# The last product of a gated block, formed by one level of Strassen on pairs of token tiles

## The chip, the cores and the metric

The kernel runs on one core of a Trainium2 chip. The metric is the time of one execution on the device in microseconds (us); less is better. A core has TensorE (PE: matmuls, with their weight loads shown apart as PEld), VectorE (DVE), ScalarE (ACT), GpSimd (POOL) and SyncE (SP), which issues the DMA transfers here. Each engine takes its instructions in the order in which they stand in its queue and waits on semaphores.

## What is computed

Two branches work on the same normalised input, and their product is added to it (S = 2048 tokens, D = 576, Fh = 2304):

```python
xn = _layernorm(x, axis=-1)
s = _A_ref(xn, A_wqkv, A_wo)          # 32 heads, sliding window of 256, then @ wo
# _B_ref:
z = _gelu(xn @ w_in)                  # [S, 2 * Fh]
z1 = z[..., :Fh]
z2 = _layernorm(z[..., Fh:], axis=-1)
g = jnp.einsum("ts,bsf->btf", w_sp, z2) + b_sp[None, :, None]
b = jnp.einsum("bsf,fd->bsd", z1 * g, w_out)     # the last product
return x + s * _silu(b)
```

All inputs are float32. The kernel splits every float32 operand into a high part h (rounded to the matmul format by ACT) and a low part l (the rest, by a subtraction), and forms a product of two operands as three matmuls: h h, h l, l h. This is what `split` does.

## The kernel before

The kernel goes through its stages one after the other; TensorE has work in all of them.

- First come the projections and attention (the first half of the span), the product with `wo`, and at the side the first product of the gate branch. Its results lie in DRAM: `z1_d`, `z2_d`, and the attention branch's result in `s_d`.
- **The spatial stage** (L1205 to L1430) multiplies `w_sp` with z2. It already uses one level of Strassen: `PRODUCTS` names seven products of 1024 x 1024 blocks. The features go in three groups g of 384; per group there are 7 products n, each in 8 steps s of 128 rows, so `order_sp` holds 168 steps m. A step is 18 matmuls of 128x512 into six PSUM banks `acc`. `load_w` fetches the `w_sp` operand four steps ahead, `split_step` splits it two steps ahead. `evict` adds a product's banks to the running sums when its last step (s = 7) is done, and queues the gate's remaining work in `lazy`: loads of z1, Gelu, the multiplication with z1, and the stores of the result y = z1 * g into `y_d` (features on rows, tokens on columns). `run_lazy(4)` takes four of these in each step.
- In the last group w_out is made ready at the side: `wout_unit` loads one of its 18 row blocks (128 x 576) and splits it. The places are buffers that the spatial stage no longer needs (`w_place`, `last_weights`). `y_ahead` and `y_second` do the same with the first two token tiles of y.
- **The out stage** (L1432 to L1494) takes the 16 token tiles in eight chunks of two. `load_y` loads a chunk of y (256 tokens, 1 KB pieces) and splits it. For each token tile there are 18 feature blocks x 3 matmuls of the split x 2 halves of 288 output columns, all 128x288, accumulated in two PSUM banks (`po`). Four such pairs of banks are in rotation, so a tile's banks are read while the next tile's are filled. `finish_half` then applies Silu, multiplies with a row block of `s_d`, adds x, and the result is stored.

The spatial stage's order on all engines is the order of the program (`manual_schedule`); in the out stage a planner had set it. SP's queue, too, is one queue: a transfer that waits for its buffer holds back all later ones.

The lines of the profile that the text uses: L1396 the spatial matmuls (`acc`), L1489 the out-stage matmuls (`po`), L114 and L115 the two halves of `split` (ACT, DVE), L1345 and L1326 sums and multiplication of the gate, L1332 the stores to `y_d`, L1445 the loads of y, L1476 to L1478 the three steps of `finish_half`. L684, L270 and L836 to L840 are GpSimd's additions in earlier stages.

Of the kernel before, what the change touches and what calls it, by code (L numbers as in the profile page):

```python
# [9 lines left out]
F32 = mybir.dt.float32  # L10
# [6 lines left out]
P = 128  # L17
# [47 lines left out]
def kernel(  # L65
# [30 lines left out]
    s_d = dram.tile([S, D], F32, name="s_d")  # L96

# [115 lines left out]
    raws, halves, wpools = {}, {}, []  # L213

# [19 lines left out]
    with ExitStack() as early:  # L234
# [889 lines left out]
        wpools.append(open_pool(ctx, "w0p", side="right"))  # L1124
        with ExitStack() as ph:
# [39 lines left out]
            for n in range(NS):  # L1165
# [26 lines left out]
                if n == 13:  # L1192
                    thirds.close()
                    wpools.append(open_pool(ctx, "sprp", bufs=2, side="right"))
# [9 lines left out]
    zq = open_pool(ctx, "zq")  # L1204
    with ExitStack() as ph:  # L1205
        wpools.append(open_pool(ph, "wsp", bufs=2, side="right"))
        wk = open_pool(ph, "wk", bufs=2)
        accp = open_pool(ph, "accp", space=PSUM)
# [9 lines left out]
        wos = {}  # L1218
        wbufs = []
        y_first, y_raw = {}, []  # L1220

        def y_ahead():

            raws = []

            def load(j):
                raw = wk.tile([P, 512], F32, name=f"u2{j}", bufs=1).rearrange("p (f t) -> p f t", t=P)
                n = min(4, FH // P - 4 * j)
                sp.dma_start(raw[:, :n], y_d[4 * j * P:(4 * j + n) * P, 0:P].rearrange("(f p) t -> p f t", p=P))
                raws.append((raw, n))  # L1230

            def form(j):
                raw, n = raws[j]
                for i in range(n):
                    f = 4 * j + i
                    c0 = 4 * D + f % 3 * 2 * P
                    h, l = (wbufs[f // 3][:, c0 + a * P:c0 + a * P + P] for a in range(2))
                    split(h, l, raw[:, i])
                    y_first[f] = (h, l)

            return [partial(load, j) for j in range(5)], [partial(form, j) for j in range(5)]

        def wout_unit(f, place):

            def load():
                raw = wk.tile([P, D], F32, name="wr")
                sp.dma_start(raw, w_out[f * P:(f + 1) * P, :])
                return raw

            def form(raw):  # L1250
                hl = place()
                for h in hl[0]:
                    w = h.shape[-1]
                    c0 = 0 if h is hl[0][0] else 288
                    act.activation(h, raw[:, c0:c0 + w], AF.Copy)
                whole = [tuple(h[:, a * 288:a * 288 + 288] for a in range(2)) if len(hs) == 1 else hs
                         for hs in map(tuple, hl) for h in hs[:1]]
                for l in hl[1]:
                    w = l.shape[-1]
                    c0 = 0 if l is hl[1][0] else 288  # L1260
                    if w == D and len(hl[0]) == 1:
                        dve.tensor_tensor(l, raw, f32(hl[0][0]), ALU.subtract)
                    else:
                        for a in range(c0 // 288, (c0 + w) // 288):
                            b = a * 288
                            dve.tensor_tensor(l[:, b - c0:b - c0 + 288], raw[:, b:b + 288], f32(whole[0][a]),
                                              ALU.subtract)
                wos[f] = whole

            return load, form  # L1270

        def w_place(n, k, i):

            if i == 0:
                wbufs.append((xp if k < 5 else zc).tile([P, 8 * ZW], F32R, name=f"b{k}"))
            return [[wbufs[n][:, (2 * i + a) * D:(2 * i + a + 1) * D]] for a in range(2)]

        places = []

        def last_place(i):  # L1280
            if not places:
                places.extend(last_weights())
            return places[i]

        def last_weights():

            r = [w_tile(len(order_sp) + n, [P, 1024], F32R, "spr") for n in range(3)]
            h, l = (w_tile(len(order_sp), [P, 1024], F32R, t) for t in ("sph", "spl"))
            z = w_tile(len(order_sp), [P, ZW], F32R, "zh")
            lead, rest = slice(0, D), slice(D, D + 288)  # L1290
            return [([r[0][:, lead]], [r[1][:, lead]]), ([r[2][:, lead]], [h[:, lead]]),
                    ([l[:, lead]], [r[0][:, rest], r[1][:, rest]]),
                    ([r[2][:, rest], h[:, rest]], [l[:, rest], z[:, :288]])]

        def y_second():

            for j in range(6):
                raw = zq.tile([P, ZW], F32, name="zr", bufs=ZRB).rearrange("p (f t) -> p f t", t=P)
                sp.dma_start(raw, y_d[3 * j * P:3 * (j + 1) * P, P:2 * P].rearrange("(f p) t -> p f t", p=P))
                y_raw.append(raw)  # L1300

        def tiles(name):
            return [wk.tile([P, 512], F32, name=f"{name}{j}", bufs=1) for j in range(6)]
# [262 lines left out]
```

## Time and profile before

| | |
|---|---|
| median of 3 runs | 1881.53 us (1880.1 to 1881.65) |
| the profiled execution | 1876.21 us, span 1874.5 us |
| mean granted TensorE clock | 0.997 |
| busy: PE, PEld, DVE, ACT, POOL | 98%, 86%, 56%, 49%, 21% |
| spatial stage | about 953 to 1640 us |
| out stage | 1640 to 1870 us, 1728 matmuls |

The busy share of PE says little by itself: matmuls are pipelined, so that one of 295 ns starts every 133 ns, and their durations overlap. What counts is the distance between starts and whether TensorE waits. The share on the chain of waits is a better guide. POOL has no work after the first half of the span.

### The profile page before, as it was taken

Reading aid. Unit: us, or ns where it says so; the run is one execution under the profiler, and the core shown is the slowest. Engines: PE = TensorE matmul, PEld = TensorE weight load, DVE = VectorE, ACT = ScalarE, POOL = GpSimd, SP = SyncE. Lnnn points to the kernel's source line nnn. Section 1 sums busy time; section 2 is a strip of 40 time slices with the busy share of each in tenths; the row PEclk is TensorE's granted clock in tenths of the full one; section 3 lists DMA queues with packets and bytes.
Section 4 is the critical chain, followed back from the end, with each engine's and each line's share of the span. In section 5 each row is a group of like instructions: output and inputs, shape, how many; then the busy total and the mean of one; then the engine's idle time right before and its main releaser. Section 6 shows DMA issues by size and latency. Waiting matters only on the chain.

```text
span 1874.5 us, 38529 instructions
## 1 busy us (share of the span) xinstructions
PE 1845.2 (98%) x14552; PEld 1613.9 (86%) x14552; DVE 1040.6 (56%) x2273; ACT 914.3 (49%) x1760; POOL 399.8 (21%) x487
## 2 busy tenths in 40 slices
PE   8999999999999999999999999999999999999999
PEld 8999999997777777776988888888888888899998
DVE  6311333457766776751257686667857666653322
ACT  5523222315666676666467655565465434532221
POOL 3332333434465455554000000000000000000000
PEclk8999999999999999999999999999999999999999
DMA  7895688886566676655867668566586547765441
GB/s 250 205 231 164 229 288 280 287 273 192 161 193 168 174 200 181 181 144 171 259 226 255 237 218 291 210 230 203 197 285 204 192 144 230 252 215 168 135 134 60
DMA packets 234314, 389.85 MB, mean 208 GB/s; under 512 B 51984, under 2 KB 145680, under 8 KB 234000
## 3 DMA queue, kind: packets, MB, share of 16 engines
q1 hardware_dynamic: 234128, 387.39, 65.8%
q8 instruction: 114, 1.87, 0.4%
q14 instruction: 72, 0.59, 0.1%
HBM read 274.74 MB, written 111.78 MB: 206 GB/s over the span
## 4 chain that ended last, share of the span: by engine, by line
PE 87%; DVE 4%; DMA 3%; SPq 2%; ACT 2%; issue 1%; POOL 0%; POOLq 0%; DVEq 0%; ACTq 0%
PE acc L1396 34%; PE po L1489 12%; PE mb L205 11%; PE ma L669 6%; PE mb L669 5%; PE ma L205 5%; PE ops L750 4%; PE tps L722 3%; PE sp L598 3%; PE wops L1155 2%; SPq L361 1%; DMA st_d<-qkhl 1%; DMA att<-st_d 1%; PE ma L378 1%; DVE junk L602 1%
## 5 line engine op out<-in xcount | busy, mean ns | idle before, releaser
L1396 PE MATMUL acc<-spl,zh 128*128 128x512 f32 x1008 | 392.6, 389 | 0.8 <-DVE spl L115 0.6
L1396 PE MATMUL acc<-sph,zh 128*128 128x512 f32 x1008 | 392.2, 389 | 0.0
L1396 PE MATMUL acc<-sph,zl 128*128 128x512 f32 x1008 | 392.2, 389 | 0.0
L602 DVE CUSTOM_DVE_ANT_0 junk<-sp,band 128x384 bf16<-128x384 f32 (+1 forms) x512 | 276.2, 540 | 111.6 <-PE sp L598 32.9
L726 ACT ACTIVATE pt<-tps 128x384 f32<-128x384 f32 (+2 forms) x576 | 231.3, 441 | 120.4 <-PE tps L722 76.5
L669 PE MATMUL mb<-b,z1wh 64*128 64x512 f32 x648 | 224.7, 399 | 1.0 <-ACT z1o L674 0.6
L1396 PEld LDWEIGHTS acc<-spl,zh 128*128 128x128 f32 x1008 | 189.2, 188 | 41.7 <-DVE spl L115 2.4
L669 PE MATMUL ma<-b,z1wh 64*128 64x512 f32 x648 | 223.8, 397 | 0.6 <-ACT zt L946 0.4
L1396 PEld LDWEIGHTS acc<-sph,zl 128*128 128x128 f32 x1008 | 189.2, 188 | 39.2
L1396 PEld LDWEIGHTS acc<-sph,zh 128*128 128x128 f32 x1008 | 189.2, 188 | 39.1
L115 DVE TENSOR_TENSOR spl<-spr,sph 128x1024 fp32r<-128x1024 f32 x168 | 205.4, 1223 | 30.0 <-ACT sph L114 29.0
L114 ACT ACTIVATE zh<-b 128x384 fp32r<-128x384 f32 x168 | 87.4, 520 | 228.8 <-PE acc L1396 228.6
L722 PE MATMUL tps<-att 56*128 56x384 f32 (+1 forms) x576 | 176.6, 344 | 2.8 <-DMA att<-mhl 1.3
L115 DVE TENSOR_TENSOR zl<-b,zh 128x384 fp32r<-128x384 f32 x168 | 93.1, 554 | 152.0 <-ACT zh L114 152.0
L114 ACT ACTIVATE sph<-spr 128x1024 fp32r<-128x1024 f32 x168 | 175.8, 1047 | 0.6 <-DMA spr<-in_w_sp_dram 0.5
L598 PE MATMUL sp<-att 54*128 54x384 f32 (+1 forms) x512 | 160.8, 348 | 2.1 <-DVE mx L602 2.1
L1489 PE MATMUL po<-b,yh 128*128 128x288 f32 x840 | 147.2, 295 | 0.5 <-ACT gs L1476 0.5
L669 PE MATMUL ma<-b,z1wl 64*128 64x512 f32 x324 | 128.0, 395 | 0.0
L669 PE MATMUL mb<-b,z1wl 64*128 64x512 f32 x324 | 127.4, 393 | 0.0
L722 PEld LDWEIGHTS tps<-att 56*128 56x128 f32 x576 | 99.4, 184 | 30.9 <-issue 9.0
L1489 PEld LDWEIGHTS po<-b,yh 128*128 128x128 f32 x840 | 124.1, 188 | 0.7 <-ACT gs L1476 0.7
L669 PEld LDWEIGHTS ma<-b,z1wh 64*128 64x128 f32 x648 | 117.2, 186 | 6.9 <-ACT z1o L674 1.8
(229 smaller groups left out, 4163.3 us busy)
## 6 DMA issues: line engine op xcount, KB each, us to landing
spr<-sc_d SPq DMA_DIRECT2D x96, 512.0 KB
spr<-in_w_sp_dram SPq DMA_DIRECT2D x72, 512.0 KB
zr<-z_d SPq DMA_DIRECT2D x144, 192.0 KB
z_d<-zt SPq DMA_DIRECT2D x48, 384.0 KB
z_d<-z1o SPq DMA_DIRECT2D x72, 256.0 KB
z1t<-z_d SPq DMA_DIRECT2D x72, 256.0 KB
y_d<-z1t SPq DMA_DIRECT2D x72, 256.0 KB
a<-in_w_sp_dram SPq DMA_DIRECT2D x64, 256.0 KB
```

Source lines behind the costliest of these rows:

```text
L114: act.activation(hi, src, AF.Copy)
L115: dve.tensor_tensor(lo, src, f32(hi), ALU.subtract)
L205: pe.matmul(banks[h][:, :n], *both[h][i], start=i == 0, stop=i == STEPS - 1)
L598: pe.matmul(ps[:, :w], q_of(u, j)[0:54, i * P:(i + 1) * P], k_of(u, j)[0:54, k0:k0 + w], start=True, stop=True)
L602: dve.tensor_tensor_reduce(out=junk[:, :w], in0=ps[:, :w], in1=band[:, m0:m0 + w], scale=1.0, scalar=-3.0e38, op0=ALU.add, op1=ALU.max, ac ...
L669: pe.matmul(ps, w, x_, start=n == 0, stop=n == STEPS - 1)
L722: pe.matmul(ps[:, :m * P], k_of(u, j)[:, (kb - base) * P:(kb - base + 1) * P], q_of(u, j)[:, (a - lo) * P:(a - lo + m) * P], start=True, s ...
L726: act.activation(pt[:, j, d0:d0 + n * P], ps[:, (qa - a) * P:(qa - a + n) * P], AF.Exp, scale=scale)
L750: pe.matmul(o_ps[c][32 * j:32 * j + 32, (qa - 4 * c) * P:(hi - 4 * c + 1) * P], vgs[u][:, kb - k0, j * VW:j * VW + 32], pt[:, j, (qa - kb) ...
L1155: pe.matmul(po[:, i, :288], lt[:, cs], r[:, i * 288:(i + 1) * 288], start=n == 0, stop=n == len(pl) - 1)
L1396: pe.matmul(acc[j], z[:, ps], w[:, cs], start=s == i == 0 and n in OPENS, stop=s == 7 and i == 2, skip_group_check=True)
L1489: pe.matmul(po[i][:, a, :288], y if ahead else y[:, i * P:(i + 1) * P], w[a], start=f == 0 and m == 0, stop=f == NF - 1 and m == 2)
```

## The change

The last product is formed by one level of Strassen (in Winograd's form). A pair p is made of two token tiles t and t + 4; y is cut into quarters a11, a12 (tile t, first and second half of the features) and a21, a22 (tile t + 4), w_out into four quarters of 1152 x 288. Instead of eight products of quarters there are seven, in the order `W_ORDER` = P4, P1, P2, P6, P7, P5, P3, each 9 feature blocks x 3 matmuls of 128x288.

- The four sums of weight quarters are formed by GpSimd in group 1 of the spatial stage (`t_load`, `t_form`, `t_store`) and stored to DRAM as `t_d`.
- The seven weight operands are 63 blocks of 128 x 288. `w_fetch` loads five at a time (tiles 0 to 12), `w_halve` splits them: ACT forms the high part, DVE or, where `pool` is given, GpSimd the low part. Tiles 0 to 6 are halved in group 2 of the spatial stage, tile 7 in its last step, tiles 8 to 12 during the first two products of the out stage.
- `y_load` loads a quarter of a pair in three transfers (128 tokens, 512-byte pieces); `y_form` splits a product's operand (three pieces of 384 columns) and has GpSimd form the sums of quarters in place: six additions after P4's split, three after P1's, three after P2's.
- In PSUM, P2 is added onto P1's bank, P7 onto P6's and P3 onto P5's. `total` reads a bank after its product: ACT copies P4 and P1 to SBUF (`t4`, `t1`), DVE adds the others to running sums. `end` applies Silu and the rest to a quarter of the output; `load_end` loads the rows for it two quarters ahead.
- After each product i, the order on every engine's queue is: `total(i)`, `formed(i + 3)` (the split for the product three further, and the load of the next pair's quarter that takes its buffer), at i = 0 and 1 the weights, then `end`.
- The whole out stage is now in program order as well.

In the diff below the removed functions (`y_ahead`, `wout_unit`, `w_place`, `last_place`, `last_weights`, `y_second`, and the old out stage) are cut.

```diff
...
+        def t_form(t, n):
+            b11, b12, b21, b22 = (t[:, m, :n] for m in range(4))
+            pool.tensor_tensor(b11, b12, b11, ALU.subtract)
+            pool.tensor_tensor(b12, b22, b12, ALU.subtract)
+            pool.tensor_tensor(b22, b22, b11, ALU.subtract)
+            pool.tensor_tensor(b21, b21, b22, ALU.subtract)
...
+        W_ORDER = ("P4", "P1", "P2", "P6", "P7", "P5", "P3")
+        W_SUMS = {"P5": 0, "P6": 1, "P7": 2, "P4": 3}
+        W_PARTS = {"P1": (0, 0), "P2": (1, 0), "P3": (1, 1)}
...
+        def w_fetch(i, home):
+            n = 3 if i == 12 else 5
+            raw = (home.tile([P, 2304], F32, name=f"o{i % 2}") if home is yw else
+                   home.tile([P, 1440], F32, name="wr", bufs=2))
...
+        def w_halve(i, home, name, low=dve):
+            raw = w_raws.pop(i)
+            n = raw.shape[1]
+            t = home.tile([P, 8 * ZW if home in (xp, zc) else n * D], F32R, name=name)[:, :n * D]
+            t = t.rearrange("p (a k c) -> p a k c", a=2, c=288)
+            act.activation(t[:, 0], raw, AF.Copy)
+            low.tensor_tensor(t[:, 1], raw, f32(t[:, 0]), ALU.subtract)
+            w_tiles.append(t)
...
+        QUADS = ("a11", "a21", "a22", "a12")
+        OF = {"P4": "a22", "P1": "a11", "P2": "a12", "P6": "a11", "P7": "a21", "P5": "a22", "P3": "a12"}
...
+        def y_form(i, p, prod):
+            home = yw if i % 3 < 2 else homes["o2"]
+            o = home.tile([P, 2304], F32R, name=f"o{i % 3}", bufs=1).rearrange("p (a f t) -> p a f t", a=2, t=P)
+            src = quads[p, OF[prod]]
+            for n in range(3):
+                split(o[:, 0, 3 * n:3 * n + 3], o[:, 1, 3 * n:3 * n + 3], src[n])
+            operands[p, prod] = o
+            q = {name: quads.get((p, name)) for name in QUADS}
+            if prod == "P4":
+                for n in range(3):
+                    pool.tensor_tensor(q["a22"][n], q["a21"][n], q["a22"][n], ALU.add)
+                    pool.tensor_tensor(q["a21"][n], q["a11"][n], q["a21"][n], ALU.subtract)
...
             if s == 7:
-                evict(g, n)
+                evict(g, n, acc)
             load_w(m + 4)
             split_step(m + 2)
...
+            if g == 1 and n < 5:
+                k0, w = 2 * n, 1 if n == 4 else 2
+                if s == 1:
+                    t_now = t_load(k0, w)
+                if s == 3:
+                    t_form(t_now, w)
+                if s == 6:
+                    t_store(t_now, k0, w)
...
+                if n == 6:
+                    if s == 2:
+                        y_load(0, "a11")
+                        y_load(0, "a21")
+                    if s == 3:
+                        y_load(0, "a22")
+                        y_load(0, "a12")
+                    if s in (5, 6):
+                        y_form(s - 5, *SEQ[s - 5])
...
+        OPEN_OF = {"P4": "P4", "P1": "P1", "P2": "P1", "P6": "P6", "P7": "P6", "P5": "P5", "P3": "P5"}
...
+        def product(i):
+            p, prod = SEQ[i]
+            key = p, OPEN_OF[prod]
+            begin = key not in banks
+            if begin:
+                banks[key] = outp.tile([P, 512], F32, name=f"c{len(opened) % 8}", bufs=1)
+                opened.append(key)
+            o = operands.pop((p, prod))
+            for k in range(9):
+                wh, wl = w_block(prod, k)
+                for n, (y, w) in enumerate(((o[:, 0, k], wh), (o[:, 0, k], wl), (o[:, 1, k], wh))):
+                    pe.matmul(banks[key][:, :288], y, w, start=begin and k == n == 0, stop=k == 8 and n == 2,
+                              skip_group_check=True)
+            return banks[key][:, :288]
...
+        for i in range(len(SEQ)):
+            c = product(i)
+            done = total(i, c)
+            formed(i + 3)
+            if i == 0:
+                w_halve(8, right, "w0", pool)
+                w_fetch(9, right)
+                w_fetch(10, right)
+                run_lazy(len(lazy))
+                gates.close()
+                yp = open_pool(ph, "yp")
+                for _ in range(2):
+                    load_end()
+                w_halve(9, right, "w1", pool)
+                w_fetch(11, right)
+            if done is not None:
+                end(i, done)
+                load_end()
+            if i == 1:
+                w_halve(10, yp, "w2")
+                w_fetch(12, right)
+                w_halve(11, yp, "w3", pool)
+                w_halve(12, yp, "w4", pool)
```

306 lines of the change are left out of this document (144 added, 162 removed).

## The prediction

> **What bounds the kernel now.** I read the page first, then the chain of waits, then the last 250 us as a timeline and in windows. The page:
>
> ```profile
> span 1874.5 us, 38529 instructions
> ```
> ```profile
> PE 87%; DVE 4%; DMA 3%; SPq 2%; ACT 2%; issue 1%; POOL 0%; POOLq 0%; DVEq 0%; ACTq 0%
> ```
> ```profile
> L115 DVE TENSOR_TENSOR spl<-spr,sph 128x1024 fp32r<-128x1024 f32 x168 | 205.4, 1223 | 30.0 <-ACT sph L114 29.0
> L114 ACT ACTIVATE zh<-b 128x384 fp32r<-128x384 f32 x168 | 87.4, 520 | 228.8 <-PE acc L1396 228.6
> ```
> ```profile
> L115 DVE TENSOR_TENSOR zl<-b,zh 128x384 fp32r<-128x384 f32 x168 | 93.1, 554 | 152.0 <-ACT zh L114 152.0
> L114 ACT ACTIVATE sph<-spr 128x1024 fp32r<-128x1024 f32 x168 | 175.8, 1047 | 0.6 <-DMA spr<-in_w_sp_dram 0.5
> ```
>
> TensorE carries 87% of the chain. The end of that chain is the stage that is rewritten, and one window inside that stage:
>
> ```profile
> 1640.20 222.22 PE po L1489 x1674
> ```
> ```profile
> 1862.91 7.47 PE po L1489 x54
> ```
> ```profile
> 1740.00:1760.00 20.00, 20.00 (x153) 20.00 (x152) 8.79 (x14) 6.39 (x10) 0.00 (x0) 1.00 0.55 178
> ```
>
> The output product is 1728 matmuls back to back: 222.22/1674 = 0.1327 us from start to start, with DVE 44% busy, ACT 32%, POOL idle and the clock at 1.00. Nothing else is late there, so the stage (229.7 us) is worth exactly its matmul count. The profiled execution took 1876.2 us, 1.7 more than its span; the median of the runs shown is 1881.5, 5.3 above it. I make the sum against the profiled time and add the change to the median.
>
> **What is removed.** 16 token tiles x 18 x 3 x 2 = 1728 matmuls become 8 pairs x 7 products x 27 = 1512 of the same 128x288 shape, each with its own weight load as before. 216 x 0.1327 = 28.7 us less. One product is 27 x 0.1327 = 3.58 us.
>
> **What is added inside each pair.** Before, a product had its own two banks and nobody had to empty them in time. Now P2 adds onto P1's bank, P7 onto P6's and P3 onto P5's, and each must wait until ACT (t1) or DVE has read the bank, straight after its last matmul. The end of the kernel shows such a reading, and step 167 of the spatial stage shows TensorE released by DVE:
>
> ```profile
> 1870.08 0.29 PE L1489 MATMUL po<-sph,yl 128*128 128x288 f32 x1
> 1870.40 0.41 ACT L1476 ACTIVATE gs<-po 128x288 f32<-128x288 f32 x1 [7.55 <-PE po L1489]
> 1870.85 0.46 DVE L1477 TENSOR_TENSOR fs<-fs,gs 128x288 f32<-128x288 f32 x1 [7.01 <-ACT gs L1476]
> ```
> ```profile
> 1634.75 1.22 DVE L115 TENSOR_TENSOR spl<-spr,sph 128x1024 fp32r<-128x1024 f32 x1 [0.39 <-ACT sph L114]
> ```
> ```profile
> 1636.03 0.19 PEld L1396 LDWEIGHTS acc<-spl,zh 128*128 128x128 f32 x1 [0.32 <-DVE spl L115]
> ```
>
> The next matmul would have started at 1870.21; ACT reads 1870.40 to 1870.81, TensorE resumes 0.06 later: 0.65 us lost. With DVE's 0.46 it is 0.70. Before P3 DVE has also to finish P7's two sums, P4's three subtracts and P7's multiply and add; that is 2 x 0.46 + 3 x 0.48 (next rows) + 2 x 0.46 = 3.3, with the waits for ACT's copies and Silu between them about 4, against the 3.58 of P5: I take 0.5 more. 0.65 + 0.70 + 1.20 = 2.55 us a pair, 20.4 us in all. Bounds: 2.05 a pair (16.4) if DVE is always free; above, the port rival below.
>
> Each pair also has 21 splits of 384 columns, 12 POOL adds, 12 loads of y, 8 row loads, 4 stores:
>
> ```profile
> 1652.10 2.60 ACT L114 ACTIVATE yh<-zr 128x384 fp32r<-128x384 f32 x6 [1.36 <-DVE z1t L1326]
> 1652.91 2.90 DVE L115 TENSOR_TENSOR yl<-zr,yh 128x384 fp32r<-128x384 f32 x6
> ```
> ```profile
> L684 POOL TENSOR_TENSOR z1wl<-z1raw,z1wh 128x384 fp32r<-128x384 f32 x51 | 51.1, 1025 | 6.7 <-ACT z1wh L684 6.7
> ```
> ```profile
> L270 POOL TENSOR_TENSOR wql<-wraw,wqh 128x1152 fp32r<-128x1152 f32 x13 | 34.7, 2677 | 60.4 <-ACT wqh L267 49.1 <-DVE xpair L318 9.9 <-ACT qkhl L114 1.4
> ```
>
> ACT: 21 x 0.43 + 6 readings of 0.41 = 11.5 us. DVE: 21 x 0.48 + 13 x 0.46 = 16.1. POOL: 12 x 1.02 = 12.3. A pair lasts 7 x 3.58 + 2.55 = 27.6 us, so on totals these lie beside TensorE and cost nothing more.
>
> **The start of the stage.** This is the dear place. Weights 7 to 12 are no longer formed under the spatial stage: their fetch and halving stand in the queues of SP, ACT, DVE and POOL during the first pair, in program order, and ahead of the bank readings. The rows for the walk:
>
> ```profile
> 1642.97 3.67 DVE L1345 TENSOR_TENSOR cb<-acc,t 128x512 f32<-128x512 f32 x6
> ```
> ```profile
> 1647.97 2.49 DVE L1326 TENSOR_TENSOR z1t<-z1t,cb 128x512 f32<-128x512 f32 x4
> 1648.68 4.49 SPq L1332 DMA_DIRECT2D y_d<-z1t  x6
> ```
> ```profile
> 1656.19 1.45 SPq L1445 DMA_DIRECT2D yr<-y_d  x3
> ```
> ```profile
> 1659.46 0.85 ACT L114 ACTIVATE yh<-yr 128x768 fp32r<-128x768 f32 x1 [4.76 <-DMA yr<-y_d]
> ```
> ```profile
> 1662.01 1.28 ACT L1476 ACT_TABLE_LOAD   x1
> ```
> ```profile
> 1632.00:1634.00 2.00, 2.00 (x11) 1.65 (x10) 0.20 (x1) 1.91 (x4) 0.00 (x0) 1.00 1.11 346
> ```
>
> Prices: an issue on SP 0.48; transfer at 0.35 MB/us; landing 1.7 after transfer (3.27 from issue to use, less 0.48 and 393 KB/0.35 = 1.1). Halving 1440 columns: by the 384 and 1024 rows ACT 1.39, DVE 1.66; by the 384 and 1152 rows POOL 3.30.
>
> Time 0 is the end of the spatial stage (1640.0). DVE came free of the last split at -4.0. It then does nine operand subtracts (4.3, and about 2 for POOL's adds beside them), weight 7 (1.7), the six sums of the last gate (3.7), four multiplies (2.5) and P6's three subtracts (1.5): 11.7. Only these free the buffers of a11, so SP issues the next pair's a11 until 13.1 and weight 9's fetch until 13.6. 0.59 + 0.74 MB from 12.2 on take 3.8 us; it lands at 17.7. ACT halves it (19.1), and only behind that reads P1's bank (19.5). P2 was due at 2 x 3.58 + 0.65 = 7.8: **11.7 us late**. P2 and P6 end at 26.7. Meanwhile SP issues weight 10, six stores (4.5) and four row loads until 21; weight 11 waits for POOL's low half of weight 9 (19.1 + 3.3 = 22.4) and goes out by 22.9, three loads of a21 by 24.3, weight 12 by 24.8. These 1.77 MB, from 22.9 on, have landed at 29.7. ACT halves weight 12 (0.9), copies P5's operand (1.3), loads its table (1.3), does Silu (0.4); DVE multiplies and adds (0.9) and only then reads P6's bank (0.5): P7 starts at 35.0, due at 27.4: **7.6 late**. Together 19.3 us. Before, sums, multiplies and stores of the last gate ran on until 1653 as well (rows above), under matmuls that waited for none of it; that cover is gone, because P2 and P7 wait for engines which have this work ahead. Bounds: 2 if the weights land before ACT reaches them, 32 if every landing takes half as long again and POOL slows DVE throughout.
>
> TensorE's own clock follows such pauses:
>
> ```profile
> 10.00:15.00 5.00, 2.98 (x38) 2.62 (x40) 2.86 (x8) 2.57 (x5) 2.62 (x2) 0.65 0.66 261
> 15.00:20.00 5.00, 5.00 (x62) 5.00 (x64) 3.55 (x11) 3.26 (x7) 2.72 (x3) 0.67 0.58 203
> ```
>
> After 2 us of idleness the granted clock is 0.65 and 0.67. In five us at 0.67 a third is lost, 1.7 us. The first pause pays nothing, since P7 waits for the weights anyhow; the second pays 1.7. The Trainium skill, "TensorE: Matmul & The Clock Gate", Part 1, says that an idle window of about 3.4 us puts the clock to half until a busy window has passed. By that rule the estimate is the same 1.7 for each pause.
>
> **Smaller edits.** The sums of w_out on GpSimd lie in group 1 of the spatial stage, five times four adds of up to 576 columns and 40 transfers; DVE there is
>
> ```profile
> 1301.00:1376.00 75.00, 75.00 (x333) 62.12 (x332) 54.57 (x80) 39.79 (x60) 0.00 (x0) 1.00 0.61 207
> ```
>
> 73% busy and the DMA engines 61%, which hides them; the seven weights halved in group 2 take places that w_out's rows had. But the last split already came 0.32 us late (row above) and now has six y loads more ahead on SP: +1, between 0 and 5. The last product has one DVE sum more: +0.5.
>
> **Sum.** -28.7 + 20.4 + 19.3 + 1.7 + 1 + 0.5 = +14.2 us: 1890.4 for the profiled execution, 1895.7 for the median.
>
> **Rivals.** *The start is covered* (the other side). If weights 9 to 12 land before ACT's queue reaches them, the start costs 2, and with the lower bound for the banks -28.7 + 16.4 + 2 + 0.5 = -9.8: 1871.7 for the median. It decides once the start costs under 8. For it: DMA rows of 0.35 MB/us and buffers that may come free sooner than I walk; against it: the order on SP, which has a11's loads ahead of weight 9.
>
> *DVE and POOL hold each other up.* Around 228 us, where both work, the trace shows it:
>
> ```profile
> 223.58 1.47 DVE L115 TENSOR_TENSOR z2w<-z1wl,z2w 128x384 fp32r<-128x384 f32 x3
> ```
> ```profile
> 227.53 3.78 DVE L115 TENSOR_TENSOR z2w<-z1wh,z2w 128x384 fp32r<-128x384 f32 x3
> ```
> ```profile
> 227.84 1.49 POOL L837 TENSOR_TENSOR a<-a,a 128x512 f32<-128x512 f32 x1
> ```
> ```profile
> 244.82 1.29 POOL L836 TENSOR_TENSOR a<-a,a 128x512 f32<-128x512 f32 x1 [12.36 <-DMA a<-in_w_sp_dram]
> ```
>
> Beside POOL's adds three subtracts take 3.78 instead of 1.47. If that meets P4's subtracts and P7's multiply and add in every pair, the reading of P5's bank comes 2.3 us later, 8 x 2.3 = 18 more than the forecast: 1914. Against it: POOL's six adds start only behind those subtracts. The Trainium skill, "SBUF — State Buffer", section Who interferes with whom, says that a VectorE instruction with two SBUF inputs and a GpSimd one that reads SBUF exclude each other for a whole instruction. The trace agrees in part: DVE slows to 39%, POOL only to 87%.
>
> **How the numbers follow.** A measurement of this kernel tells about 0.2%, 3.8 us, from no change. The forecast (start 12 to 28 us late) has 0.58, the port rival 0.14, a start that costs 4 to 8 and ends near zero 0.08, the covered start 0.20. So faster 0.20, same 0.08, slower 0.72. The forecast alone reaches from 1886 to 1905. The range goes down to the covered start at 1873 and up to 1911, leaving out its lower half and most of the port rival.
>
> **What would show it.** Right: about 1512 matmuls at 0.133; in the first pair, pauses of near 12 us before P2 and 8 before P7; then pairs of 27 to 28 us with three pauses of 0.6 to 1.3 each, released by ACT and DVE. Wrong: a first pair under 35 us, pauses in the spatial stage over 5 us, or later pairs over 29 us.

## The result, and the profile after

| | before | after |
|---|---|---|
| median of 4 runs beside each other | 1880.82 us (1879.06 to 1881.65) | 1926.01 us (1920.23 to 1929.66) |
| ratio | | 1.0239, interval 1.0212 to 1.0266 |
| the profiled execution | 1876.21 us, span 1874.5 | 1929.66 us, span 1928.0 |

The changed kernel is 2.4% slower, 45 us; forecast were 14 us slower. 1926.0 lies above the range (1873 to 1911). The sign was right, the size was not.

The page of the changed kernel, its span, busy times, granted clock by slices and chain:

```profile
span 1928.0 us, 38834 instructions
...
PE 1840.4 (95%) x14336; PEld 1601.7 (83%) x14336; DVE 1184.4 (61%) x2404; ACT 960.1 (50%) x1872; POOL 561.0 (29%) x607
...
PEclk9999999999999999999999999999999999789999
...
PE 83%; DVE 7%; DMA 4%; issue 3%; ACT 2%; SPq 1%; POOL 0%; DVEq 0%; ACTq 0%; POOLq 0%
```

PE is on 83% of the chain instead of 87%, DVE on 7% instead of 4%. The out stage (L1503 here, operation `c`) begins at 1647.4 and lasts 280.6 us to the end of the span; before, it began at 1640.0 and lasted 234.5: 46.1 more. The spatial stage lasts 688.5 us instead of 687.4; the rest of the 53.5 us between the two spans is a spatial stage that begins 6.3 us later (958.9 instead of 952.6). The edit leaves the work up to there as it was, and the other kernels of this study began it at 952.4 to 957.8: that part is put down to the spread between executions.

The out stage on TensorE, as a timeline: start, time, engine, line, operation, count, and in brackets the wait ahead of the group and what ended it. The first pair and the two after it:

```profile
1647.37 7.29 PE L1503 MATMUL c<-b,o 128*128 128x288 f32 x54
1674.21 9.22 PE L1503 MATMUL c<-b,o 128*128 128x288 f32 x54 [19.55 <-ACT t L1511]
1693.15 3.22 PE L1503 MATMUL c<-b,o 128*128 128x288 f32 x12 [9.71 <-DVE u2s L1516]
...
1705.55 5.38 PE L1503 MATMUL c<-w,o 128*128 128x288 f32 x27 [2.50 <-DVE u3s L1525]
...
1718.58 7.40 PE L1503 MATMUL c<-b,o 128*128 128x288 f32 x54 [0.50 <-ACT t L1511]
1726.62 1.83 PE L1503 MATMUL c<-b,o 128*128 128x288 f32 x12 [0.64 <-ACT o L115]
...
1736.51 5.26 PE L1503 MATMUL c<-w,o 128*128 128x288 f32 x27 [2.51 <-DVE u3s L1525]
...
```

The pauses stand where the forecast had put them: before P2 (ACT's copy of P1's bank), before P7 (DVE's u2s; for 1726.62 the profile names the last semaphore, an operand of ACT, but DVE read the bank just then) and before P3 (u3s). The first pair is far too long, and the later ones take 30.7 to 31.0 us from P3 to P3 (1736.51 - 1705.55 = 31.0), not 27.6. The wait of 2.51 was put at 1.20, and behind it the 27 matmuls of P3 are shown with 5.26 us, where they have 3.80 at full clock (the time shown runs to the end of the last matmul; from start to start it is 3.6). The clock shows why; windows by stretch (busy times of PE, PEld, DVE, ACT, POOL, then clock, DMA share, GB/s):

```profile
1736.50:1767.40 30.90, 27.24 (x190) 26.61 (x190) 24.24 (x35) 11.53 (x28) 14.62 (x13) 0.94 0.46 135
...
1736.50:1740.00 3.50, 3.49 (x15) 3.50 (x16) 3.50 (x4) 0.40 (x1) 3.42 (x4) 0.54 0.44 126
```

Behind the pause the granted clock is 0.54 for 3.5 us, and 0.51 to 0.58 behind that of every other pair but the last. VectorE is busy for 24.2 us in the pair, where its instructions by themselves add up to 16.1. What it does ahead of u3s, and GpSimd at that time:

```profile
1762.19 2.30 DVE L116 TENSOR_TENSOR o<-u,o 128x384 fp32r<-128x384 f32 x3
1764.41 1.26 DVE L1533 TENSOR_TENSOR sv<-sv,gs 128x288 f32<-128x288 f32 x1
1765.71 1.14 DVE L1534 TENSOR_TENSOR xr<-xr,sv 128x288 f32<-128x288 f32 x1
1766.77 0.44 DVE L1525 TENSOR_TENSOR u3s<-c,u3s 128x288 f32<-128x288 f32 x1
```
```profile
1762.82 1.26 POOL L1311 TENSOR_TENSOR u<-zr,u 128x384 f32<-128x384 f32 x1 [15.50 <-DVE o L116]
...
```

GpSimd's sums begin as soon as the first of the three subtracts has released its piece. The multiply and the addition of P7's end, 0.46 each in the profile of before, take 1.26 and 1.14; u3s, which reads PSUM, keeps its 0.44.

The start, as timelines of ACT, SP and DVE:

```profile
1672.46 1.40 ACT L1275 ACTIVATE w<-wr 128x1440 fp32r<-128x1440 f32 x1 [14.06 <-DMA wr<-t_d]
1673.77 0.39 ACT L1511 ACTIVATE t<-c 128x288 f32<-128x288 f32 x1
```
```profile
1665.33 1.42 SPq L1297 DMA_DIRECT2D zr<-y_d  x3
1666.85 1.00 SPq L1267 DMA_DIRECT2D wr<-t_d  x2
```
```profile
1649.36 3.95 DVE L116 TENSOR_TENSOR o<-u,o 128x384 fp32r<-128x384 f32 x3
1653.45 2.25 DVE L1276 TENSOR_TENSOR b<-wr,b 128x1440 fp32r<-128x1440 f32 x1
...
1659.21 4.38 DVE L1347 TENSOR_TENSOR z1t<-z1t,cb 128x512 f32<-128x512 f32 x2
```

ACT stands 14 us before weight 9, and P1's bank is read behind that. Weight 9 is fetched at 1666.85, 19.5 us after the spatial stage (forecast 13.6), behind y's loads, which wait for buffers that DVE frees. And DVE is slow beside GpSimd's sums of the first pair: three subtracts take 3.95 instead of 1.45, two multiplies 4.38 instead of 1.25. That this is only a part of the lateness is shown by the first experiment.

### The profile page after: what moved, and what is told of

It is laid out like the page before. It is cut to its first block, busy times and chain, and to the rows that moved or that the text cites. A ratio compares the mean times of both kernels' runs of the same rounds, so it can differ in the third digit from the quotient of the medians.

```text
span 1928.0 us, 38834 instructions
## 1 busy us (share of the span) xinstructions
PE 1840.4 (95%) x14336; PEld 1601.7 (83%) x14336; DVE 1184.4 (61%) x2404; ACT 960.1 (50%) x1872; POOL 561.0 (29%) x607
## 4 chain that ended last, share of the span: by engine, by line
PE 83%; DVE 7%; DMA 4%; issue 3%; ACT 2%; SPq 1%; POOL 0%; DVEq 0%; ACTq 0%; POOLq 0%
PE acc L1417 32%; PE mb L206 11%; PE c L1503 8%; PE ma L206 7%; PE ma L671 6%; PE mb L671 5%; PE ops L752 4%; PE tps L724 3%; PE sp L600 2%; PE wops L1157 2%; DVE o L116 1%; DMA z1t<-z_d 1%; DVE junk L604 1%; DMA zr<-z_d 1%; PE ma L380 1%
## 5 line engine op out<-in xcount | busy, mean ns | idle before, releaser
L116 DVE TENSOR_TENSOR spl<-spr,sph 128x1024 fp32r<-128x1024 f32 x168 | 209.5, 1247 | 38.5 <-ACT sph L115 37.5
L1417 PEld LDWEIGHTS acc<-sph,zl 128*128 128x128 f32 x1008 | 189.2, 188 | 39.3
L116 DVE TENSOR_TENSOR zl<-b,zh 128x384 fp32r<-128x384 f32 x168 | 99.4, 592 | 127.4 <-ACT zh L115 127.4
L1503 PE MATMUL c<-b,o 128*128 128x288 f32 x960 | 135.5, 300 | 37.3 <-ACT t L1511 23.1
L1503 PEld LDWEIGHTS c<-b,o 128*128 128x128 f32 x960 | 131.1, 192 | 40.9 <-ACT t L1511 24.9
L1311 POOL TENSOR_TENSOR u<-zr,u 128x384 f32<-128x384 f32 x24 | 30.4, 1268 | 405.1 <-DVE o L116 389.5
L736 POOL TENSOR_SCALAR_AFFINE_SELECT pt<-pt 128x512 f32<-128x512 f32 x128 | 81.7, 638 | 181.2 <-ACT pt L728 175.8
L949 DVE BATCH_NORM_STATS2 st<-zt 128x6 f32<-128x384 f32 x96 | 49.2, 547 | 131.3 <-ACT zt L948 131.2
```

The lines of the kernel that those rows point to most:

```text
L116: dve.tensor_tensor(lo, src, f32(hi), ALU.subtract)
L736: pool.affine_select(out=pt[:, :, 0:P], in_=pt[:, :, 0:P], pattern=[[0, 4], [1, P]], compare_op=ALU.is_ge, fill=0.0, base=0, channel_multi ...
L1417: pe.matmul(acc[j], z[:, ps], w[:, cs], start=s == i == 0 and n in OPENS, stop=s == 7 and i == 2, skip_group_check=True)
L1503: pe.matmul(banks[key][:, :288], y, w, start=begin and k == n == 0, stop=k == 8 and n == 2, skip_group_check=True)
```

## The experiments

Two theories stood against each other for the later pairs (GpSimd's sums slow VectorE's instructions; or the shared banks and VectorE's place in the order), two for the start (the late weights; or VectorE's work and the order). Ratios are against runs of the kernel before on the same chip (1879.0 to 1880.7 us).

### Without GpSimd's sums

```diff
-            if prod == "P4":
-                for n in range(3):
-                    pool.tensor_tensor(q["a22"][n], q["a21"][n], q["a22"][n], ALU.add)
 ...            (all twelve additions of a pair)
```

> Leaves out the twelve GpSimd additions of each pair, so the products P6, P7, P5 and P3 use unsummed quarters of y; all else stays. Port theory (DVE's subtracts, multiply and add are slow beside POOL's additions, so P5's bank is read late): the wait before P3 falls from 2.5 us to 0.7, the clock stays at 1.00 in the pairs after the first, and a pair falls from 30.8 to 27.5 us; with a first pair some 8 us shorter the time falls by about 30 us, to 1896. Rival (operands come late from DMA and SP): pairs stay at 30 to 31 us, and the time within 5 us of 1926.

1902.82 us, ratio 1.0130 (1.0113 to 1.0148), against 1.0239 with the sums. TensorE and DVE in a later pair:

```profile
1727.88 3.80 PE L1492 MATMUL c<-w,o 128*128 128x288 f32 x27 [0.64 <-ACT o L115]
...
1755.40 1.82 PE L1492 MATMUL c<-w,o 128*128 128x288 f32 x12 [0.64 <-ACT o L115]
```
```profile
1752.09 1.49 DVE L116 TENSOR_TENSOR o<-u,o 128x384 fp32r<-128x384 f32 x3
1753.50 0.45 DVE L1522 TENSOR_TENSOR sv<-sv,gs 128x288 f32<-128x288 f32 x1
```

The pair takes 27.5 us, the wait before P3 is 0.64, P3 takes its 3.80: the forecast's pair of 27.6, to a tenth. So the twelve sums cost 3.3 us a pair: 1.87 in the wait and the rest in the clock.

The time fell by 23 us and not by the 30 expected, since the first pair gained little. There are no sums beside it either, and yet P2 begins 25.3 us after the spatial stage (1646.8), 17.5 late instead of 19.0, and P3 53.6 us after it instead of 58.2. DVE, then TensorE:

```profile
1653.09 1.66 DVE L1276 TENSOR_TENSOR b<-wr,b 128x1440 fp32r<-128x1440 f32 x1 [4.25 <-ACT b L1275]
```
```profile
1672.12 9.95 PE L1492 MATMUL c<-b,o 128*128 128x288 f32 x54 [18.02 <-ACT t L1500]
```

VectorE is fast now, and stands idle for 4.25 us before weight 7. The fetch of its rows goes out at 1647.01, behind the last spatial matmul, for which SP had waited, and ACT can halve them only at 1651.65. So weight 7 is late whether VectorE is slow or not, and most of the start's lateness stays without the sums.

### An own bank for each product

```diff
-        OPEN_OF = {"P4": "P4", "P1": "P1", "P2": "P1", "P6": "P6", "P7": "P6", "P5": "P5", "P3": "P5"}
+        OPEN_OF = {prod: prod for prod in W_ORDER}
```

> Gives each of the seven products a bank of its own, so the sums P1+P2, P6+P7 and P5+P3 in PSUM are left out, and no product waits for a reading of its bank. Bank theory (only the three readings hold TensorE up): a pair falls to 25.1 us, the clock stays at 1.00, the time falls by 7 x 5.7 = 40 us and some 5 more from the first pair, to about 1881. Throughput theory (DVE beside POOL is itself the bound: it is busy about 25 of a pair's 30.8 us): the pair stops at 27 us or more, because operands come late instead, and the time ends near 1895.

1895.26 us, ratio 1.0094 (1.0079 to 1.0109). No product waits for a bank any more, GpSimd's sums are there, and the pair still takes 27.4 us, by a window over one:

```profile
1738.91 5.17 PE L1503 MATMUL c<-b,o 128*128 128x288 f32 x37 [0.77 <-DVE o L116]
```
```profile
1734.30:1761.70 27.40, 25.54 (x190) 25.07 (x190) 24.06 (x35) 11.35 (x28) 14.71 (x12) 1.00 0.52 152
```

VectorE, slowed by GpSimd, is busy for 24.1 of 27.4 us, and TensorE waits for low halves (L116) instead. Without its bank waits a pair could last 25.1 us; it is no shorter than with bank waits and without the sums. Behind the wait stands VectorE.

### Silu, multiply, addition and store one product later

```diff
-            if done is not None:
-                end(i, done)
-                load_end()
+            if waiting_end is not None:
+                end(*waiting_end)
+                load_end()
+            waiting_end = (i, done) if done is not None else None
```

> Computes everything. Silu, multiply, add and store of a quarter stand one product later in the queues, behind the next product's reading of its bank. Port theory: P5's reading no longer stands behind P7's multiply and add (1.25 + 1.15 us beside POOL), the wait before P3 falls from 2.5 to under 1 us, the clock stays up, a pair falls by about 3.3 us to 27.5, and the time by 23 us to about 1903. Rival (the order within DVE's queue is not what delays the reading): the pair stays within 1 us of 30.8 and the time within 8 us of 1926.

1918.85 us, ratio 1.0218 (1.0195 to 1.0242): 7 us less instead of 23, a miss. Pairs take 29.5 us on average, and the wait before P3 is 0.64 in some and 2.1 to 3.4 in the others. There the operand that stands ahead of the bank's reading waits for its load of y, as ACT's timeline shows:

```profile
1757.60 1.69 ACT L115 ACTIVATE o<-u 128x384 fp32r<-128x384 f32 x3 [4.87 <-DMA u<-y_d]
```

The stores have moved to a later place in SP's queue, with loads of y behind them. That they are what delays these loads was not tried by itself.

### The multiply and the addition with one input in PSUM

The two PSUM banks for this are taken from the products, which turn over six instead of eight.

```diff
...
-            gs = yp.tile([P, 288], F32, name="gs", bufs=2)
+            gs = outp.tile([P, 512], F32, name=f"g{len(ends) % 2}", bufs=1)[:, :288]
             act.activation(gs, c, AF.Silu)
-            dve.tensor_tensor(sv, sv, gs, ALU.mult)
-            dve.tensor_tensor(xr, xr, sv, ALU.add)
+            dve.tensor_tensor(gs, sv, gs, ALU.mult)
+            dve.tensor_tensor(xr, xr, gs, ALU.add)
```

> Silu's result and its product with the gate row lie in two PSUM banks instead of SBUF, the products turn over the other six banks. The multiply and the addition of each end then have one input in SBUF and one in PSUM; GpSimd's sums stay. Theory (a VectorE instruction is slowed beside GpSimd only when both its inputs are in SBUF): the multiply and the addition take 0.46 again instead of 1.26 and 1.14, the three subtracts keep their 2.3, P5's bank is read about 1.5 us earlier, the wait before P3 is 1.0 to 1.3 and the clock dips no more: 30.8 - 1.4 - 1.6 = 27.8 a pair, 1905. If the clock still dips, 29.4 a pair, 1916. Rival (any VectorE instruction that touches SBUF is slowed beside GpSimd): multiply and addition stay above 0.9 and the pair at 30 or more, 1921 or more.

1906.13 us, ratio 1.0134 (1.0110 to 1.0159). DVE, and GpSimd beside it:

```profile
1755.76 2.30 DVE L116 TENSOR_TENSOR o<-u,o 128x384 fp32r<-128x384 f32 x3
1757.98 0.45 DVE L1533 TENSOR_TENSOR g<-sv,g 128x288 f32<-128x288 f32 x1
1758.46 0.45 DVE L1534 TENSOR_TENSOR xr<-xr,g 128x288 f32<-128x288 f32 x1
```
```profile
1757.72 1.20 POOL L1312 TENSOR_TENSOR zr<-zr 128x384 f32<-128x384 f32 x1
```

In the same microseconds as an addition of GpSimd, the two instructions take 0.45 each, and the three subtracts, with both inputs in SBUF, their 2.30 as before. The wait before P3 is 1.02, the clock stays at 1.00, a pair takes 27.9 us. So what slows a VectorE instruction is an addition of GpSimd beside it together with a second input in SBUF, and not GpSimd's presence as such. The Trainium skill, "SBUF — State Buffer", section Who interferes with whom, has the rule: VectorE and GpSimd share one pair of SBUF ports under an exclusive lock, and a VectorE instruction needs it for a second SBUF input. These rows agree on the second input; the lock itself they do not show.

### GpSimd's sums on VectorE

For pairs 1 to 7 VectorE makes the twelve sums, placed where it has time.

```diff
+            if prod == "P6":
+                y_sum(p, "a11", "a22", "a11", ALU.subtract)
+            if prod == "P7":
+                y_sum(p, "a12", "a12", "a11", ALU.subtract)
             y_form(i, p, prod)
...
+            if i % 7 == 5:
+                y_sum(i // 7 + 1, "a22", "a21", "a22", ALU.add)
+            if i % 7 == 6:
+                y_sum(i // 7 + 1, "a21", "a11", "a21", ALU.subtract)
```

> For pairs 1 to 7 the twelve sums of y a pair are made by VectorE instead of GpSimd: the sum for P5 behind P5's own product, that for P7 behind P3's, those for P6 and P3 while P4 and P1 of the pair run, where VectorE has least to do. Pair 0 stays as it is. Theory (GpSimd's adds slow VectorE's, and the pause that this makes before P3 also lowers the clock): VectorE has 16.0 + 12 x 0.5 = 22 us of work in a pair but each of its additions takes 0.5 again, so the wait before P3 falls from 2.5 to about 0.7, the clock stays at 1.00 and a pair takes 27.2 to 27.8 instead of 30.8: 7 x 3.3 = 23 us less, near 1904. Rival (VectorE's total is what counts, whoever slows it): 22 us of work in a pair with two readings of banks in its queue leaves pairs of 29 to 30 us and a time of 1914 to 1920, with waits released by VectorE's low halves.

1902.36 us, ratio 1.0117 (1.0102 to 1.0131). A window from P3 to P3:

```profile
1727.87:1755.31 27.44, 25.66 (x189) 25.01 (x190) 21.43 (x46) 11.59 (x28) 0.00 (x0) 1.00 0.52 152
```

With twelve instructions more, VectorE is busy for 21.4 us in a pair instead of 24.2. GpSimd's help cost VectorE more than the work it took over.

### What the clock does behind a pause

On that version, n idle additions read P5's bank ahead of its real reading, n rising or falling over pairs 1 to 7. GpSimd does nothing there.

```diff
+            if prod == "P5":
+                junk = small[p, "t1"]
+                for _ in range((0, 1, 2, 3, 4, 5, 6, 8)[p]):
+                    dve.tensor_tensor(junk, c, t, ALU.add)
```

> The version with VectorE's sums for pairs 1 to 7, whose wait before P3 is 0.64 us at a clock of 1.00, with 1, 2, 3, 4, 5, 6 and 8 idle additions of VectorE ahead of the reading of P5's bank in pairs 1 to 7: they read the bank and write a row that nobody reads, so they only lengthen that one wait, by about 0.4 to 0.5 us each, from 1.1 to 4.5 us. GpSimd does nothing there. Theory (a pause of about 2.4 us before P3 by itself lowers the clock for some 3.5 us, as in the changed kernel): P3 takes 3.6 us behind pauses under about 2 us and 5.0 to 5.3 behind those from 2.4 on. Rival (the clock falls only with GpSimd's adds beside it, or by something else in the pair): P3 takes 3.6 us behind the pauses of 2.4 to 3 too.

> The same with 8, 6, 5, 4, 3, 2 and 1 idle additions in pairs 1 to 7. If the length of the pause decides, P3's time goes by the number of additions as in the run with rising numbers, in the opposite order of pairs. If what decides is where the pause falls in a window that runs by itself, the same number of additions gives a slow P3 in one run and a fast one in the other, in the middle of the row (2 to 4 additions).

1928.84 us (ratio 1.0261, 1.0215 to 1.0306) and 1924.69 us (1.0239, 1.0193 to 1.0284). The row of pauses was the same in both, from 1.13 to 4.58 us. Two of them in the run with rising numbers:

```profile
1758.53 3.80 PE L1510 MATMUL c<-w,o 128*128 128x288 f32 x27 [1.62 <-DVE u3s L1536]
...
1787.48 5.34 PE L1510 MATMUL c<-w,o 128*128 128x288 f32 x27 [2.12 <-DVE u3s L1536]
```

And in the run with falling numbers:

```profile
1856.53 5.36 PE L1510 MATMUL c<-w,o 128*128 128x288 f32 x27 [2.12 <-DVE u3s L1536]
...
1886.61 3.81 PE L1510 MATMUL c<-w,o 128*128 128x288 f32 x27 [1.62 <-DVE u3s L1536]
```

In both orders pauses of 1.13 and 1.62 left the clock at 1.00, and those of 2.12 and more halved it for 3.4 us or longer. So the pause alone does it, without GpSimd. Yet length isn't all of it: a pause of 4.58 halved it for 6.8 us in one run and for 3.4 in the other, and with the ends one product later P3 ran at 1.00 behind a pause of 2.71,

```profile
1732.14 3.81 PE L1503 MATMUL c<-w,o 128*128 128x288 f32 x27 [2.71 <-ACT o L115]
```

and behind 2.13 it did not. The kept traces show what decides. In each of them the stretches at half clock last 3.41 us or a whole multiple of it (but for one that outlasts the work at the kernel's end), and they begin whole multiples of 3.41 us apart. In the changed kernel those of the later pairs begin at 1736.32, 1767.04, 1797.76 and so on, 30.72 us or nine times 3.41 apart; pairs of 30.7 to 31.0 us meet nearly the same place each time. Time is cut here into such stretches, by windows: first around the pause of 2.12 above, then around that of 2.71:

```profile
1785.31:1788.73 3.42, 1.30 (x10) 1.28 (x10) 3.22 (x8) 1.79 (x4) 0.00 (x0) 1.00 0.48 134
1788.73:1792.14 3.41, 3.41 (x17) 3.41 (x16) 2.25 (x6) 0.00 (x0) 0.00 (x0) 0.50 0.28 87
```
```profile
1727.60:1731.01 3.41, 1.83 (x14) 1.59 (x13) 2.02 (x3) 1.68 (x4) 1.99 (x2) 1.00 0.97 285
1731.01:1734.43 3.42, 2.29 (x17) 2.32 (x18) 3.42 (x5) 1.47 (x4) 3.34 (x4) 1.00 0.21 56
```

TensorE is idle for 2.1 us of the first stretch, and the next has half the clock. The longer pause lies across two stretches, with 1.6 us in one and 1.1 in the other, and costs nothing. In the out stages of the changed kernel and of the twelve experiments, a stretch at full clock with 1.9 us of idleness or more was followed by one at half clock each time (60 of them), one with 1.72 or less never; the two between, with 1.77 and 1.78, went one each way. So a pause costs when it takes up more than about half of such a stretch. The Trainium skill, "TensorE: Matmul & The Clock Gate", Part 1, tells of a free-running window of about 3.4 us that has to be idle. The free-running window agrees with these rows; an idle time of 3.4 us was not needed, 2.12 sufficed.

### The start without its late weights

Tiles 8 to 12 are not fetched and halved; tiles 0 to 4 stand in for them.

```diff
-                w_halve(8, right, "w0", pool)
-                w_fetch(9, right)
-                w_fetch(10, right)
+                w_raws.pop(8)
+                w_tiles.extend(w_tiles[:5])
```

> Weight tiles 8 to 12 are neither fetched nor halved; tiles 0 to 4 stand in for them, so parts of P7, P5 and P3 use wrong weights. Start theory (the late weights hold the bank readings of the first pair): P3 of the first pair, which begins 58 us after the stage's start instead of 24, begins at about 34, and the time falls by about 24 us to 1902; later pairs stay at 30.8. Rival (the last gate's sums and multiplications on DVE beside POOL are what delays the first pair): P3 of the first pair begins at 48 or later, and the time falls by less than 10 us.

1907.87 us, ratio 1.0161 (1.0137 to 1.0185): 18 us less. The first pair:

```profile
1654.38 4.12 PE L1503 MATMUL c<-b,o 128*128 128x288 f32 x29 [2.81 <-ACT t L1511]
...
1671.56 9.77 PE L1503 MATMUL c<-b,o 128*128 128x288 f32 x54 [8.71 <-DVE u2s L1516]
1683.83 6.34 PE L1503 MATMUL c<-b,o 128*128 128x288 f32 x35 [2.50 <-DVE u3s L1525]
```

P3 begins 39.5 us after the spatial stage (1644.3), against 58.2 with the late weights and 24.0 when nothing is late. The late weights cost 18.6 of the 34 us; most of the other 15 lies before P7, behind VectorE's queue.

### The start in order of need

Weights 9 and 10 are fetched ahead of y, the banks' readings stand ahead of the halvings, Silu and the stores behind; VectorE makes the low halves of weights 8 and 9.

```diff
             if i == 0:
-                w_halve(8, right, "w0", pool)
+                run_lazy(4)
+                w_halve(7, zc, "b5")
                 w_fetch(9, right)
-                w_fetch(10, right)
+            if i == 1:
+                w_halve(8, right, "w0")
+                w_fetch(10, right)
+                formed(3)
+                formed(4)
...
```

> The same work, with the queues of the first pair put in order of need: weight 7 is halved after the last gate's sums, the readings of the banks stand ahead of the halvings, weights 9 and 10 are fetched ahead of the next pair's y, Silu and the stores stand behind what the next products wait for, and VectorE makes the low halves of weights 8 and 9. The operands of P6 and P7 are formed one product later. GpSimd's sums of pair 0 stay. Theory (order in the queues makes the start late, as the run without late weights says for 18.6 of 34 us): the first P3 starts 30 to 38 us after the spatial stage instead of 58, and the time is 20 to 27 less, 1900 to 1906; later pairs stay at 30.8. Rival (the memory comes free too late and transfers and halving set the start, whatever the order): the first P3 starts at 48 or later and the gain is under 10 us, 1916 or more.

1920.48 us, ratio 1.0214 (1.0199 to 1.0228): 5.5 us less, a miss.

```profile
1652.86 4.09 PE L1505 MATMUL c<-b,o 128*128 128x288 f32 x29 [0.50 <-ACT t L1513]
1661.67 6.03 PE L1505 MATMUL c<-b,o 128*128 128x288 f32 x25 [4.72 <-DVE o L116]
1677.78 3.20 PE L1505 MATMUL c<-b,o 128*128 128x288 f32 x12 [10.07 <-DVE u2s L1518]
...
1695.46 4.93 PE L1505 MATMUL c<-w,o 128*128 128x288 f32 x19 [5.66 <-POOL w L1278]
```

P2 is on time now, and the wait moves on to P6, P7 and P3. P3 begins (at 1689.04) 44.0 us after the spatial stage instead of 58.2, between the two cases expected, and it waits again in its middle: the pair ends 56.1 us after the spatial stage instead of 63.4. With VectorE's sums as well:

> VectorE's sums for pairs 1 to 7 and the start in order of need together. If the two losses are separate, their gains add up: 23 + 20 to 27 less than the changed kernel, 1876 to 1883, level with the kernel before within 0.3%. If one hides the other (a slower first pair gives the rest time to fill up, or VectorE's fuller queue holds the start), the gain is under 35 us: 1891 or more.

1893.51 us, ratio 1.0071 (1.0058 to 1.0083), by its time on the side of the second case. But neither loss hides the other: alone the two steps bring 24 and 5.5 us, together 32.5. The gain is under 35 because the new start alone brought 5.5 and not the 20 to 27 that were expected of it. In that run SP and DVE show what holds it:

```profile
1644.62 16.26 SPq L1268 DMA_DIRECT2D wr<-t_d  x5
```
```profile
1675.18 0.46 DVE L1542 TENSOR_TENSOR sv<-sv,gs 128x288 f32<-128x288 f32 x1 [7.18 <-DMA sv<-s_d]
...
```

Weight 9 waits for the place of weight 7's raw rows, and u2s (at 1676.05) stands behind the end of P2, which waits 7 us for its row.

### Another order of the products, and the start again

The version with both steps gets the order P1, P4, P2, P6, P5, P7, P3. A product now lies between any two that share a bank; ACT copies P5's result out, and P5's sum is made after P7.

```diff
-        W_ORDER = ("P4", "P1", "P2", "P6", "P7", "P5", "P3")
+        W_ORDER = ("P1", "P4", "P2", "P6", "P5", "P7", "P3")
...
-            if prod in ("P4", "P1"):
+            if prod in ("P4", "P1", "P5"):
                 act.activation(small_tile(p, "t" + prod[1]), c, AF.Copy)
```

> The version with VectorE's sums and the start in order of need, with the seven products in another order: P1, P4, P2, P6, P5, P7, P3. Between two products that share a bank there is now another product, and P5's result is copied out by ScalarE as those of P1 and P4 are, so no product follows on a bank that has just been read. Theory (what is left of a later pair beyond its matmuls is the three readings of banks, 0.50 + 0.64 + 0.64 and 0.2 of hand-over each): the three waits go and a pair takes 25.1 to 25.8 instead of 27.5, 7 x 2 = 14 us less than the version before it, 1877 to 1881. Rival (VectorE, with 23 us of work in 25, cannot keep up): waits for its low halves take their place, pairs stay at 26.5 or more and the time at 1887 or more.

1876.36 us, ratio 0.9989 (0.9977 to 1.0001), a little under what was expected: no wait for a bank is left in the later pairs. In the first, P7 still waits 6.0 us for P6's bank. Then the start, with places of their own for the raw rows of weights 9 and 10, and with P2's end behind P5:

```diff
+                t = wk.tile([P, 3072], F32, name="t1")
+                w_fetch(9, None, t[:, :1440])
+                w_fetch(10, None, t[:, 1440:2880])
```

> The version with the new order of products, with the start changed again: the raw rows of weights 9 and 10 go to the place of the last gate's sums instead of waiting for those of 7 and 8, the last gate's sums stand ahead of P2's operand on VectorE, its multiplies stand behind P6's reading, and P2's end behind P5. In the run with the start in order of need, fetches waited 16 us for those places, and the reading of P6 stood 7 us behind a row for P2's end. Theory: the first P3 starts 24 to 30 us after the spatial stage instead of 45 to 50, so with pairs of 25.1 to 25.8 the time is 1860 to 1868, 0.7 to 1.1% under the kernel before. Rival (VectorE's own work, 23 us from the end of the spatial stage to P3's last weight, beside GpSimd's sums of pair 0, holds the start): the first P3 starts at 35 or later and the time is 1870 or more.

1871.69 us, ratio 0.9960 (0.9947 to 0.9973): this version beats the kernel before by 0.4%, though not by the 0.7 hoped for: the time lies on the rival's side (1870 or more), and the first P3, at about 30 us, at the edge of what the theory gave it (24 to 30). TensorE in the first pair, and a window over pairs 2 to 6:

```profile
1669.68 0.61 PE L1519 MATMUL c<-cb,o 128*128 128x288 f32 x1 [3.76 <-ACT cb L1277]
...
1680.85 0.61 PE L1519 MATMUL c<-w,o 128*128 128x288 f32 x1 [3.15 <-ACT w L1277]
```
```profile
1711.75:1836.00 124.25, 124.25 (x942) 124.25 (x941) 104.49 (x229) 60.70 (x140) 0.00 (x0) 1.00 0.58 167
```

Pairs 2 to 6 are seven products back to back, 25.0 us each, TensorE busy without a gap at a clock of 1.00; pair 1 takes 27.7. The first pair ends 39.3 us after the spatial stage (1644.7 to 1684.0), 14 more than its matmuls: weights 10 and 12 are still late.

## Why the prediction was right or wrong

- **What is removed**, -28.7: right. 27 matmuls take 3.6 us, 0.133 each, wherever the clock is at 1.00; there are 1512 of them. The last version has it visible.
- **Bank waits**, 2.55 a pair: the first two terms were right (0.65 and 0.70 forecast from start to start, 0.50 and 0.64 of idle time measured, to which some 0.2 of hand-over come). The third was mis-sized: 1.20 forecast, 2.51 measured. The step that failed is the count of what VectorE does ahead of u3s, with 0.46 and 0.48 an instruction beside GpSimd's sums. Without these sums the wait was 0.64, less than forecast.
- **"DVE and POOL hold each other up"** was the rival, at 0.14. Its mechanism was right, and the reason against it was wrong: GpSimd's six additions don't start behind the three subtracts, but behind the first. Its price was 2.3 us; the wait grew by 1.87 (2.51 - 0.64).
- **The clock** was counted once, 1.7 us, behind one pause of the start. It falls in each later pair but the last: P3 takes 5.26 instead of 3.80. None was counted for the pauses of 0.65 to 1.20 in the later pairs, and the runs bear that out for those lengths (1.13 and 1.62 lose nothing); 2.51 loses 1.46. So contention costs nearly twice, in the wait and in the clock.
- **The start**, 19.3 late: mis-sized. P3 came 58.2 us after the spatial stage; without lateness 24.0. P2 was 19.0 late (forecast 11.7), since weight 9 was fetched at 19.5 us instead of 13.6 and landed at 25.1 instead of 17.7. P7 was 11.1 later still (7.6), and P7 to P3 4.0, with the clock's loss inside both. The order of steps in the walk was right; three of its terms failed. VectorE was done with P6's subtracts at 18.8 instead of 11.7: beside GpSimd the nine operand subtracts took 10.1 instead of 6.3 (with "about 2 for POOL's adds") and the four multiplies 5.6 instead of 2.5. The walk has no wait for weight 7, whose rows are fetched only behind the last spatial matmul; without GpSimd's sums VectorE waits 4.25 us for them, and P2 is still 17.5 late. And weight 9 landed 5.6 us behind its fetch instead of 4.1. Of the lateness of P3, 18.6 us went with the late weights and 4.6 with the sums. The upper bound of 32 for this start was passed by 2.
- **Smaller edits**: the spatial stage became 1.1 us longer, 1 forecast. The last pair, without a next one to form, has 0.64 before P3.
- **The sum.** For the out stage the forecast has +13.2, the traces +46.1. Of the 33 between, the later pairs bring 20.5 (213.7 us from the first to the last P3 instead of 7 x 27.6) and the start 13.1 (34.1 - 19.3 - 1.7).
- **"The start is covered"**, at 0.20, was far off; order alone did not cover it either.
- **The range** had room for one price of the port rival, at the bank's reading, and the bound of 32 for the start had GpSimd's slowing in it. Both together would have given 1895.7 + 12.7 + 18 = 1926, and the range ended at 1911. That this sum meets the measured time is in part luck: the rival's wait was less than priced, and the clock behind it, 1.46 in six of the later pairs, was in neither. (The forecast's own span is 1888 to 1904 by its terms, not 1886 to 1905.)

## What to carry to other kernels

When work is given to GpSimd, look at which VectorE instructions with two SBUF inputs run at that moment: here twelve additions on GpSimd cost VectorE more than the twelve additions take it. A product that adds onto a bank that was just filled gives part of a saving in matmuls back: with another product between, these waits were gone from the later pairs (25.0 instead of 27.5 us). Price a wait on TensorE together with the clock behind it, once it passes about 2 us, and walk the start of a stage through each queue with its buffers, not only its order.

## What the runs showed of the hardware

- Beside GpSimd's additions, a VectorE instruction with both inputs in SBUF took 2.5 to 3.5 times as long (three subtracts of 384 columns 3.95 instead of 1.45 us; two multiplies of 512 columns 4.38 instead of 1.25). GpSimd's additions took 1.2 to 1.3 instead of 1.02. With one input in PSUM nothing changed (0.45).
- TensorE's clock went by stretches of 3.41 us that run by themselves: after one at full clock in which TensorE was idle for 1.9 us or more the next had half the clock, after one with 1.72 or less it had not. So pauses of 2.12 to 3.10 us halved the clock for 3.4 us, pauses of 3.59 for 6.8, and pauses of up to 1.62 did nothing; one of 2.71 that lay across two stretches cost nothing either.
